# Queries and keys laid out by halves of the head pairs, the first block's tiles loaded two at a time into the rooms of late weights, alpha read by rows, two softmax buffers

## The chip, the core and the metric

The kernel runs on one core of one Trainium2 chip. The time is device microseconds of one launch. The kernel before was run three times: 926.99, 926.79 and 925.41 us, median 926.79. One more execution was profiled. The engines are called as the profile calls them: PE (TensorE, matmuls), DVE (VectorE), ACT (ScalarE), POOL (GpSimd) and SP (SyncE, which here only issues transfers).

## The reference

Attention over a band of 64 positions, 8 batches and 8 heads of width 64, and then a two-layer network with a leaky slope per hidden unit over all 4608 tokens. All values are fp32.

```
scores = scale * np.matmul(q, k.transpose(0, 1, 3, 2))
mask = (rel >= 0) & (rel < window)
scores = np.where(mask, scores, -1000000000.0)
scores = scores - np.max(scores, axis=-1, keepdims=True)
attn = np.exp(scores)
attn = attn / (np.sum(attn, axis=-1, keepdims=True) + 1e-09)
x = np.matmul(attn, v)                  # to [4608 tokens, 512]
h = x @ w_in                            # [4608, 2048]
g = np.maximum(h, 0.0) + alpha * np.minimum(h, 0.0)
out = g @ w_out                         # [4608, 512]
```

`w_in` and `w_out` arrive as 64-bit floats, read by the kernel as pairs of 32-bit words.

## The kernel before

**Tiles and blocks.** The 4608 tokens are 36 tiles of 128, in 9 blocks of 4. Each tile goes through `attend`, and each block through 16 `cell`s, one for each slice f of 128 hidden units. In the first block the slices f = 0 to 3 are done for tiles 0, 1 and for tiles 2, 3 apart.

**Attention of a tile** (`attend`). The heads are four pairs e; the token axis has two halves u of 64. Loads: two for keys (k, L314, 256 KB each), four for queries (q, L323, 64 KB each, in runs of 64 floats), two for values (v, L334, 256 KB each). SP issues all of them, save the four q of tile 0, which ACT issues. The rows 64u to 64u+63 of the k and q tiles hold the half u of the token axis, for all four pairs. Scores s (L350) are 16 products of 64x64 by 64x128 (32 entries in the profile); DVE adds the mask and takes the row maxima (L366, one for each pair and half, 8 for a tile); ACT does the exponentials (L372, 8); DVE the reciprocals rc (L383, L384); POOL scales the rows (L388). For the tiles 0 to 7 PE then turns the weights by transposes t (L405), and ACT or DVE copies them to pt (L410, L412); PE multiplies by v into av (L441), ACT rounds it to xh (L445), DVE makes the remainder xl (L448). From tile 8 on DVE does the turning.

**Weights** (`weights`). There are 32 of them to prepare once: 16 slices of w_in and 16 of w_out, in turn. For each: a fetch by SP of 512 KB (raw, L239), a step on the high words by ACT or DVE (two, L248 or L250), a shift on DVE (L255 or L258), a conversion of the low words on ACT (low, L263), a join on DVE (val, L267), an addition on POOL (L271), a rounding on ACT to the high part (L282), and a subtraction on POOL or DVE for the low part (L286). High and low part are kept all through the run in win_h, win_l, wout_h, wout_l.

**A cell** is the product h (L482; high by high, high by low, low by high), the slope on ACT and DVE (g, L488, L491), the split of g into gh (ACT, L496) and gl (POOL, in the first block also DVE, L500), and the product o (L515), which adds up over the 16 slices.

**What sets the order.** The kernel makes a list of steps with the engines that may do them, an expected duration, the steps that they need, and the buffers that they take and give back. `Plan.order` puts them in an order before the launch: it goes forward in time with these expected durations, and of the steps that could start next on an engine it takes the one whose latest useful time (`late`, worked back from the due times `want`) is first. The order of each engine is then fixed; an engine that meets an instruction whose data is not there waits, and all behind it waits. At most 8 transfers are in flight in the plan (`FLIGHT`).

**Buffers that matter here** (the `stock`). Two places each for k and q, one for v, one for the softmax tile w of 128 x 8 x 128 (a second one comes when the last raw weights are gone), one pt, with a second later, three for raw weights. The four kinds of weight parts are one tile each of 128 x 8192 floats.

**alpha** is read by ACT's queue with one element in a run (`"(f p) -> p f"`, 2048 runs of 4 bytes); DVE makes the signs from it in four steps (L565 to L568).

Of the kernel before, what the change touches and what calls it, by code (L numbers as in the profile page):

```python
# [143 lines left out]
PAIRS = 4  # L144
TURNS = (14, 2, 6, 10)
# [5 lines left out]
def banded_attention_then_prelu_ffn(  # L151
# [47 lines left out]
    alpha_sb = const.tile([P, NF], F32, name="alpha_sb")  # L199
# [4 lines left out]
    win_h = const.tile([P, NP, DFF], F32R, name="win_h")  # L204
    win_l = const.tile([P, NP, DFF], F32R, name="win_l")
    wout_h = const.tile([P, NF, E], F32R, name="wout_h")
    wout_l = const.tile([P, NF, E], F32R, name="wout_l")
# [3 lines left out]
    stock = dict(bank=[4, 5, 6, 7], o=[0, 1, 2, 3], q=["q0", "q1"], k=["k0", "k1"], v=["v0"], w=["w0"],  # L211
# [3 lines left out]
    stock.update({f"x{i}": [i] for i in range(RING)})  # L215
    plan = Plan(stock)
# [12 lines left out]
    def weights(c):  # L229
# [43 lines left out]
        def parts():  # L273
            v = d["val"].bitcast(F32)
            if odd:
                return v, wout_h[:, f, :], wout_l[:, f, :]
            fs = slice(f * P, (f + 1) * P)
            return v.rearrange("p (a b) -> p a b", a=NP), win_h[:, :, fs], win_l[:, :, fs]

        def high(_):  # L280
            v, hi, _ = parts()
            nc.scalar.copy(hi, v)  # L282

        def rest(e):
            v, hi, lo = parts()
            (nc.gpsimd if e == POOL else nc.vector).tensor_tensor(out=lo, in0=v, in1=hi.bitcast(F32),  # L286
                                                                  op=ALU.subtract)
# [7 lines left out]
        s6 = step({ACT: (0.51, 0.61)}, high, [s5])  # L295
        s7 = step({POOL: (1.22, 1.28), DVE: (1.15, 1.22)}, rest, [s6], give=[val])
# [6 lines left out]
    def attend(t, by_pe, want, loads_behind=(), behind=(), last=None):  # L303
# [3 lines left out]
        qb, kb, vb, wb, pb = Buffer("q", 1), Buffer("k", 1), Buffer("v", 1), Buffer("w", 2 if by_pe else 1), Buffer("pt", 1)  # L307
        loads, first_load = [], []
        for u in range(2):
            def load_k(_, u=u):  # L310
                if u == 0:
                    d["k"] = room(kb, [P, NP, 2, 2, W], F32, f"k_{t}")
                r = slice(u * D, (u + 1) * D)
                nc.sync.dma_start(d["k"][r].rearrange("d e b h w -> d e (b h w)"),  # L314
                                  kT[:, :, 2 * t + u:2 * t + u + 2].rearrange("e d b h w -> d e (b h w)"))
            loads.append(step({SP: (0.62, 0.62)}, load_k, (), [*loads_behind, *loads[:1]],
                              take=[kb] if u == 0 else [], moved=1.18))
        for u, h in ((0, 0), (0, 1), (1, 0), (1, 1)):
            def load_q(e, u=u, h=h):
                if u == h == 0:  # L320
                    d["q"] = room(qb, [P, NP, 2, W], F32, f"q_{t}")
                r = slice(u * D, (u + 1) * D)
                (nc.scalar if e == ACT else nc.sync).dma_start(  # L323
                    d["q"][r, :, h, :], qT[:, :, t, h, u * W:(u + 1) * W].rearrange("e d q -> d e q"))
            first_load.append(step({ACT if t == 0 else SP: (0.64, 0.64)}, load_q, (), [*loads_behind, *first_load[:1]],
                                   take=[qb] if u == h == 0 else [], moved=0.45))
        loads += first_load

        lv = []
        for u in range(2):  # L330
            def load_v(_, u=u):
                if u == 0:
                    d["v"] = room(vb, [P, NP, 2, P], F32, f"v_{t}")
                nc.sync.dma_start(d["v"][u * W:(u + 1) * W].rearrange("w c b d -> w c (b d)"),  # L334
                                  vN[:, :, 2 * t + u:2 * t + u + 2].rearrange("c w b d -> w c (b d)"))
            lv.append(step({SP: (0.62, 0.62)}, load_v, (), [*loads_behind, *lv[:1]], take=[vb] if u == 0 else [],
                           moved=1.18))
# [3 lines left out]
        def score(_):  # L341
            d["w"] = room(wb, [P, NH, KW], F32, f"w_{t}")
            for x in ("nm", "sm", "rc"):
                d[x] = sb.tile([P, NH], F32, tag=f"{x}{t % 2}", name=f"{x}_{t}")
            d["s"] = [bank(banks[u], [P, NP, KW], F32, f"s_{t}_{u}") for u in range(2)]
            for e in range(NP):
                for h in range(2):
                    for u in range(2):
                        r = slice(u * D, (u + 1) * D)
                        nc.tensor.matmul(d["s"][u][h * W:(h + 1) * W, e], d["q"][r, e, h, :], d["k"][r, e, :, h, :],  # L350
                                         start=True, stop=True)

        cold = 1.0 + 0.9 * (t < 2)
        sc = step({PE: (1.05 * cold, 1.15 * cold)}, score, loads, behind, take=[*banks, wb], give=[qb, kb])
# [92 lines left out]
        def x_low(_):  # L447
            nc.vector.tensor_tensor(out=xl[:, :, xs], in0=d["av"], in1=xh[:, :, xs].bitcast(F32), op=ALU.subtract)  # L448
            d.clear()
# [203 lines left out]
```

## Time and profile before

| | us |
|---|---|
| median of three runs | 926.79 |
| profiled execution | 927.84 |
| its span (first to last instruction) | 926.1 |
| PE busy | 895.6 (97%) |
| DVE busy | 452.2 (49%) |
| ACT busy | 383.8 (41%) |
| POOL busy | 310.3 (34%) |
| PE busy, 160 to 880 us | 720.00 of 720.00 |

The shares of busy time are means over two very different stages. In the first 160 us the weights are prepared and the first two blocks go through attention, and DVE, ACT and POOL have far more to do than later. From 160 us to about 918 us PE has no idle time that the profile shows. A row of a timeline gives the start and the length in us, the engine, the line, the operation, its output and inputs, the shape, how many, and in brackets the idle time of the engine before it with what ended it. A row of waits gives the engine and line that waited, for whom, the total in us, how often, and the longest.

### The profile page before, as it was taken

What the parts mean: (1) busy time and instruction counts of PE and PEld (TensorE: products, weight loads), DVE (VectorE), ACT (ScalarE), POOL (GpSimd) and SP (SyncE); (2) the same over time, 40 slices, a digit from 0 to 9 for tenths busy, and PEclk for the clock granted to TensorE, in tenths of its full rate; (3) what the DMA queues carried; (4) which work ended last, traced back from release to release, by engine and by line L of the source; (5) the groups of instructions that cost most, each with busy time, mean ns of one, the idle gap of its engine ahead of it and who ended that gap; (6) DMA issues with size and microseconds to landing.
All of it is one profiled execution on the core that took longest, in us unless ns stands there. A gap on an engine that the chain in (4) does not pass through costs nothing.

```text
span 926.1 us, 15516 instructions
## 1 busy us (share of the span) xinstructions
PE 895.6 (97%) x5872; PEld 730.0 (79%) x5872; DVE 452.2 (49%) x1317; ACT 383.8 (41%) x1020; POOL 310.3 (34%) x241
## 2 busy tenths in 40 slices
PE   3699999999999999999999999999999999999998
PEld 2578777888888888888888888888888888888886
DVE  3788996564454445444444444445444444421111
ACT  4677775433333334333333343334333433322222
POOL 3466874332333222233332233322333223322221
PEclk9999999999999999999999999999999999999999
DMA  9697756322232223111322232223222232001001
GB/s 217 171 225 198 215 158 124 96 58 57 58 104 52 54 49 97 51 45 48 100 58 57 58 103 58 58 58 103 58 57 59 57 103 57 1 1 46 1 1 46
DMA packets 96410, 74.41 MB, mean 80 GB/s; under 512 B 44624, under 2 KB 89680, under 8 KB 96336
## 3 DMA queue, kind: packets, MB, share of 16 engines
q1 hardware_dynamic: 93184, 73.16, 31.2%
q8 instruction: 46, 0.75, 0.3%
q10 hardware_dynamic: 3152, 0.27, 0.3%
q14 instruction: 28, 0.23, 0.1%
HBM read 63.97 MB, written 9.44 MB: 79 GB/s over the span
## 4 chain that ended last, share of the span: by engine, by line
PE 88%; DVE 6%; DMA 2%; issue 2%; POOL 1%; ACT 1%; SPq 0%; POOLq 0%; ACTq 0%; DVEq 0%
PE h L482 41%; PE o L515 40%; PE s L350 4%; PE av L441 4%; DVE w L366 1%; DVE val L267 1%; DMA raw<-w_out 1%; DMA raw<-w_in 1%; DVE gl L500 1%; DVE wout_l L286 1%; DVE two L255 1%; DMA q<-qT 1%; DVE two L250 1%; PE t L405 0%; POOL w L388 0%
## 5 line engine op out<-in xcount | busy, mean ns | idle before, releaser
L500 POOL TENSOR_TENSOR gl<-g,gh 128x512 fp32r<-128x512 f32 (+1 forms) x136 | 173.6, 1276 | 427.6 <-ACT gh L496 424.1
L491 DVE SCALAR_TENSOR_TENSOR g<-h,s_sb,g 128x512 f32<-128x512 f32 (+1 forms) x148 | 108.8, 735 | 290.2 <-ACT g L488 290.0
L488 ACT ACTIVATE g<-h,sa_sb 128x512 f32<-128x512 f32 (+1 forms) x148 | 100.3, 678 | 332.1 <-PE h L482 329.4
L515 PE MATMUL o<-wout_l,gh 128*128 128x512 f32 x576 | 226.6, 393 | 2.1 <-DVE wout_l L286 1.7
L515 PE MATMUL o<-wout_h,gh 128*128 128x512 f32 x576 | 226.7, 394 | 0.8 <-ACT gh L496 0.7
L426 DVE STREAM_TRANSPOSE pt<-w 32x256 f32<-32x256 f32 x336 | 146.6, 436 | 34.0 <-POOL w L388 29.2
L482 PE MATMUL h<-xh,win_h 128*128 128x512 f32 (+1 forms) x592 | 160.2, 393 | 1.8 <-DVE nm L366 1.2
L515 PE MATMUL o<-wout_h,gl 128*128 128x512 f32 x576 | 160.2, 391 | 0.6 <-POOL gl L500 0.4
L482 PE MATMUL h<-xl,win_h 128*128 128x512 f32 (+1 forms) x592 | 155.6, 385 | 0.0
L482 PE MATMUL h<-xh,win_l 128*128 128x512 f32 (+1 forms) x592 | 155.1, 384 | 0.0
L372 ACT ACTIVATE w<-w,nm 128x128 f32<-128x128 f32 x288 | 112.0, 392 | 59.5 <-DVE nm L366 59.5
L496 ACT CAST gh<-g 128x512 fp32r<-128x512 f32 (+1 forms) x148 | 90.0, 608 | 111.7 <-DVE g L491 109.6
L515 PEld LDWEIGHTS o<-wout_l,gh 128*128 128x128 f32 x576 | 108.2, 188 | 26.5 <-DVE wout_l L286 3.1
L515 PEld LDWEIGHTS o<-wout_h,gl 128*128 128x128 f32 x576 | 108.0, 188 | 25.3 <-POOL gl L500 0.9
L482 PEld LDWEIGHTS h<-xl,win_h 128*128 128x128 f32 x592 | 110.0, 189 | 22.5
L515 PEld LDWEIGHTS o<-wout_h,gh 128*128 128x128 f32 x576 | 108.2, 188 | 24.3 <-ACT gh L496 1.0
L482 PEld LDWEIGHTS h<-xh,win_l 128*128 128x128 f32 x592 | 109.9, 189 | 22.0
L482 PEld LDWEIGHTS h<-xh,win_h 128*128 128x128 f32 x592 | 107.1, 189 | 25.5 <-issue 2.1
L388 POOL TENSOR_TENSOR w<-w,rc 128x1024 f32<-128x1024 f32 (+1 forms) x44 | 70.7, 1609 | 152.3 <-DVE rc L384 142.7
L366 DVE CUSTOM_DVE_ANT_0 w<-s,masks 128x128 f32<-128x128 f32 x288 | 63.7, 286 | 63.6 <-PE s L350 63.5
L372 ACT ACTIVATION_READ_ACCUMULATOR w<-w,nm 128x1 f32 x288 | 54.6, 190 | 0.0
L350 PE MATMUL s<-k,q 64*64 64x128 f32 x1152 | 44.6, 292 | 7.9 <-DMA q<-qT 7.7
(44 smaller groups left out, 464.3 us busy)
## 6 DMA issues: line engine op xcount, KB each, us to landing
k<-kT SPq DMA_DIRECT2D x72, 256.0 KB, 4.1
v<-vN SPq DMA_DIRECT2D x72, 256.0 KB, 4.1
out<-os SPq DMA_DIRECT2D x36, 256.0 KB, 2.3
q<-qT SPq DMA_DIRECT2D x140, 64.0 KB, 3.4
raw<-w_in SPq DMA_DIRECT2D x16, 512.0 KB, 5.3
raw<-w_out SPq DMA_DIRECT2D x16, 512.0 KB, 4.7
q<-qT ACTq DMA_DIRECT2D x4, 64.0 KB, 5.4
alpha_sb<-alpha ACTq DMA_DIRECT2D x1, 8.0 KB, 5.9
```

The lines of the kernel that those rows point to most:

```text
L350: nc.tensor.matmul(d["s"][u][h * W:(h + 1) * W, e], d["q"][r, e, h, :], d["k"][r, e, :, h, :], start=True, stop=True)
L366: nc.vector.tensor_tensor_reduce(out=d["w"][:, g, :], in0=d["s"][u][:, e], in1=m, op0=ALU.add, op1=ALU.min, scale=-SCALE, scalar=3.0e38, a ...
L372: nc.scalar.activation(w, w, AF.Exp, scale=-1.0, bias=d["nm"][:, g:g + 1], accum_out=d["sm"][:, g:g + 1])
L388: nc.gpsimd.tensor_tensor(out=w, in0=w, in1=d["rc"][:, g].unsqueeze(2).broadcast_to(list(w.shape)), op=ALU.mult)
L426: nc.vector.transpose(d["pt"][ks, :, r], d["w"][r, :, ks])
L441: nc.tensor.matmul(av[r, e, u * W:(u + 1) * W], d["v"][:, e, u, r], d["pt"][:, u * NP + e, h * W:(h + 1) * W], start=True, stop=True)
L482: nc.tensor.matmul(ph[:, :nt], wt[:, c, fs], xt[:, c, xs], start=(k == 0), stop=(k == 3 * NP - 1))
L488: nc.scalar.activation(d["g"], d["h"][:, :nt], AF.Copy, scale=sa_sb[:, f:f + 1])
L491: nc.vector.scalar_tensor_tensor(out=d["g"], in0=d["h"][:, :nt], scalar=s_sb[:, f:f + 1], in1=d["g"], op0=ALU.mult, op1=ALU.max)
L496: nc.scalar.copy(d["gh"], d["g"])
L500: (nc.gpsimd if e == POOL else nc.vector).tensor_tensor(out=d["gl"], in0=d["g"], in1=d["gh"].bitcast(F32), op=ALU.subtract)
L515: nc.tensor.matmul(po[t][0], gt[:, i * P:(i + 1) * P], wt[:, f, :], start=(f == 0 and k == 0), stop=(f == NF - 1 and k == 2))
```

## The change

**Layout of q and k.** The rows 64x to 64x+63 of the tiles now hold the head pairs 2x and 2x+1, with all tokens of the tile (or two tiles) behind each other. A tile's q is two transfers with runs of 1 KB in place of four with 256 bytes; its k is two transfers of three blocks of 64 keys (384 KB in all), where the two halves before had two blocks each (512 KB). A score product still takes 64 rows by 64 queries by 128 keys; the two banks of scores now part the pairs and not the token halves.

**The first block two tiles at a time.** For tiles 0, 1 and for tiles 2, 3 one set of loads brings q, k and v of both: q 2 x 256 KB in runs of 2 KB, k 2 x 320 KB in runs of 2.5 KB, v 2 x 512 KB in runs of 2 KB. They land in rooms z0 to z3, which later become the parts of the weights with f = 12 to 15 of w_out and f = 11 to 15 of w_in (`LATE`); these parts are now tiles of their own, and the steps that write the first of each wait until the room is given back. ACT's queue issues the two k of tile 0 (behind alpha), SP all else.

**alpha by rows.** It is read as 16 rows of 512 bytes; PE turns it with one transpose (the first PE instruction, into one of the banks for o), and DVE reads it there.

**Two softmax buffers** w0 and w1 from the start.

The due time of the signs goes from 14 to 20; the high parts of a kind, and the low parts, are kept in order of f. The diff, cut to its core:

```diff
+LATE = (("wout_h", 12, "z0"), ("wout_l", 12, "z1"), ("win_h", 11, "z2"), ("win_l", 11, "z3"))
...
-    alpha_sb = const.tile([P, NF], F32, name="alpha_sb")
+    alpha_sb = const.tile([NF, P], F32, name="alpha_sb")
...
-    stock = dict(bank=[4, 5, 6, 7], o=[0, 1, 2, 3], q=["q0", "q1"], k=["k0", "k1"], v=["v0"], w=["w0"],
+    stock = dict(bank=[4, 5, 6, 7], o=[0, 1, 2, 3], q=["q0", "q1"], k=["k0", "k1"], v=["v0"], w=["w0", "w1"],
...
+    for _, _, z in LATE:
+        stock[z], stock["late " + z] = [z], []
...
-        s6 = step({ACT: (0.51, 0.61)}, high, [s5])
-        s7 = step({POOL: (1.22, 1.28), DVE: (1.15, 1.22)}, rest, [s6], give=[val])
+        prior = cv[c - 2]["done"] if c >= 2 else [None, None]
+        s6 = step({ACT: (0.51, 0.61)}, high, [s5], prior[:1] if prior[0] else [], take=late("_h"))
+        s7 = step({POOL: (1.22, 1.28), DVE: (1.15, 1.22)}, rest, [s6], prior[1:] if prior[0] else [],
+                  take=late("_l"), give=[val])
...
+        span = 2 if t < NBLK else 1
+        own = t % span
+        t0 = t - own
+        if own == 0:
+            if span == 2:
+                j = t // 2
+                qb = kb = Buffer(f"z{2 + j}", 2, f"late z{2 + j}")
+                vb = Buffer(f"z{j}", 2, f"late z{j}")
...
+            NW = 2 * span + 1
...
+                    nc.sync.dma_start(d["q"][r], qT[2 * x:2 * x + 2, :, t:t + span].rearrange("e d t h q -> d e (t h q)"))
...
+                    (nc.scalar if e == ACT else nc.sync).dma_start(
+                        d["k"][r], kT[2 * x:2 * x + 2, :, 2 * t:2 * t + NW].rearrange("e d b h w -> d e (b h w)"))
...
-                        nc.tensor.matmul(d["s"][u][h * W:(h + 1) * W, e], d["q"][r, e, h, :], d["k"][r, e, :, h, :],
-                                         start=True, stop=True)
+                            nc.tensor.matmul(d["s"][x][h * W:(h + 1) * W, u, y], q[r, y, own, h, u * W:(u + 1) * W],
+                                             k[r, y, 2 * own + u:2 * own + u + 2, h, :], start=True, stop=True)
...
-        nc.scalar.dma_start(alpha_sb, alpha.rearrange("(f p) -> p f", p=P))
+        nc.scalar.dma_start(alpha_sb, alpha.rearrange("(f p) -> f p", p=P))
+    def turn_alpha(_):
+        al["t"] = bank(ab, [P, NF], F32, "alpha_t")
+        nc.tensor.transpose(al["t"], alpha_sb, ident[:NF, :NF])
```

With other loads and buffers the plan comes out differently, on every engine, through the first two blocks. First place: SP's queue at the start of the program (k, q, v, qk are the attention's loads, raw the weights'; the number after a name is the tile's own). Before:

```order
L314 DMA k_95<-kT 64x4x256 x2
L314 DMA k_101<-kT 64x4x256 x2
L323 DMA q_106<-qT 64x4x64 x4
L334 DMA v_112<-vN 64x4x256 x2
L239 DMA raw_137<-w_in 128x4x256
L239 DMA raw_139<-w_in 128x4x256
L239 DMA raw_141<-w_out 128x1024
L314 DMA k_148<-kT 64x4x256 x2
L323 DMA q_159<-qT 64x4x64 x4
L239 DMA raw_219<-w_in 128x4x256
```

Now:

```order
L353 DMA qk_96<-qT 64x2x512 x2
L367 DMA v_101<-vN 64x4x512 x2
L249 DMA raw_104<-w_in 128x4x256
L353 DMA qk_108<-qT 64x2x512
L356 DMA qk_108<-kT 64x2x640
L353 DMA qk_108<-qT 64x2x512
L356 DMA qk_108<-kT 64x2x640
L249 DMA raw_117<-w_in 128x4x256
L249 DMA raw_141<-w_out 128x1024
L367 DMA v_173<-vN 64x4x512 x2
```

The loads of tiles 2 and 3 now stand ahead of the second raw weight; before, the first three raw weights stood ahead of tile 2's. Second place: DVE, from the end of the first masks to its first work on weights. Before (tile 0's last reciprocal, then the first weights, then the first mask of tile 1):

```order
L384 RECIPROCAL rc_118<-rc_118 128x4
L250 TENSOR_SCALAR two_183<-raw_137 128x512
L258 TENSOR_SCALAR two_183<-two_183 128x512
L267 SCALAR_TENSOR_TENSOR val_216<-raw_137,two_183 128x512
L258 TENSOR_SCALAR two_221<-two_221 128x512
L366 ISA w_194,nm_195<-s_0_198,masks 128x128
```

Now (the last mask of tile 1, whose softmax tile is w_143, then the first weight, with tile 0's copies of the turned weights, t_0 and t_1, between):

```order
L405 ISA w_143,nm_144<-s_1_148,masks 128x128
L405 ISA nm_144 128x1
L260 TENSOR_SCALAR two_206<-raw_104 128x512
L451 COPY pt_92<-t_0_195 128x512
L422 TENSOR_SCALAR rc_146<-sm_145 128x4
L423 RECIPROCAL rc_146<-rc_146 128x4
L268 TENSOR_SCALAR two_206<-two_206 128x512
L451 COPY pt_92<-t_1_214 128x512
```

Tile 1's eight masks have moved ahead of the first weight. Third place: DVE around the masks of tile 2. Before (w_309):

```order
L267 SCALAR_TENSOR_TENSOR val_291<-raw_141,two_260 128x512
L286 TENSOR_TENSOR win_l<-val_273,win_h 128x4x128
L412 COPY pt_92<-t_1_298 128x512
L258 TENSOR_SCALAR two_304<-two_304 128x512
L366 ISA w_309,nm_310<-s_0_313,masks 128x128
...
L267 SCALAR_TENSOR_TENSOR val_350<-raw_219,two_304 128x512
```

Now (w_251):

```order
L277 SCALAR_TENSOR_TENSOR val_245<-raw_104,two_206 128x512
L268 TENSOR_SCALAR two_273<-two_273 128x512
L487 TENSOR_TENSOR xl<-av_228,xh 128x4x128
L405 ISA w_251,nm_252<-s_0_255,masks 128x128
...
L265 TENSOR_SCALAR two_284<-two_284,flip_sb 128x512
L277 SCALAR_TENSOR_TENSOR val_329<-raw_117,two_273 128x512
```

One weight is joined ahead of tile 2's masks; before it was three (val_291 the third). The shift of the first w_out weight (two_284) stands right behind these masks, and all of DVE's later work behind it.

More of the change, by code (lines that the diff above doesn't have):

```diff
@@ L202, in banded_attention_then_prelu_ffn, with weight @@
     sa_sb = const.tile([P, NF], F32, name="sa_sb")
[L204 to L207, printed above, removed]
+    parts_of = {}
+    for name in ("win_h", "win_l", "wout_h", "wout_l"):
+        ends = sorted(f for n, f, _ in LATE if n == name)
+        parts_of[name] = {0: const.tile([P, ends[0], E], F32R, name=name)}
+    def weight(name, f):
+        f0 = max(x for x in parts_of[name] if x <= f)
+        return parts_of[name][f0][:, f - f0, :]
     xh = const.tile([P, NP, RING * P], F32R, name="xh")
     xl = const.tile([P, NP, RING * P], F32R, name="xl")
-    stock = dict(bank=[4, 5, 6, 7], o=[0, 1, 2, 3], q=["q0", "q1"], k=["k0", "k1"], v=["v0"], w=["w0"],
+    stock = dict(bank=[4, 5, 6, 7], o=[0, 1, 2, 3], q=["q0", "q1"], k=["k0", "k1"], v=["v0"], w=["w0", "w1"],
                  pt=["pt0"], new=[], g=["g0", "g1"], gh=["gh0", "gh1", "gh2"], gl=["gl0", "gl1"],
@@ L271, in total, with late, begin @@
             nc.gpsimd.tensor_tensor(out=d["val"], in0=d["val"], in1=d["tail"], op=ALU.add)
[L273 to L278, printed above, removed]
+        name = "wout" if odd else "win"
+        def late(part):
+            return [Buffer("late " + z, 1) for n, f0, z in LATE if (n, f0) == (name + part, f)]
+        def begin(part):
+            for n, f0, z in LATE:
+                if (n, f0) == (name + part, f):
+                    f1 = min([x for m, x, _ in LATE if m == n and x > f0], default=NF)
+                    parts_of[n][f0] = sb.tile([P, f1 - f0, E], F32R, tag=z, name=f"{n}_{f0}")
         def high(_):
-            v, hi, _ = parts()
-            nc.scalar.copy(hi, v)
+            begin("_h")
+            nc.scalar.copy(weight(name + "_h", f), d["val"].bitcast(F32))
         def rest(e):
-            v, hi, lo = parts()
-            (nc.gpsimd if e == POOL else nc.vector).tensor_tensor(out=lo, in0=v, in1=hi.bitcast(F32),
-                                                                  op=ALU.subtract)
+            begin("_l")
+            (nc.gpsimd if e == POOL else nc.vector).tensor_tensor(
+                out=weight(name + "_l", f), in0=d["val"].bitcast(F32), in1=weight(name + "_h", f).bitcast(F32),
+                op=ALU.subtract)
         s0 = step({SP: (0.4, 0.4)}, fetch, take=[raw], moved=1.3 if odd else 2.4)
@@ L306, in attend @@
         early = t < 2
[L307 to L337, printed above, removed]
+        wb, pb = Buffer("w", 2 if by_pe else 1), Buffer("pt", 1)
@@ L339, in attend @@
+        loads, lv, qb, kb, vb = st[t0]["from"]
         banks = [Buffer("o" if early else "bank", NP) for _ in range(2)]
@@ L366, in mask @@
                     nc.vector.tensor_tensor_reduce(
[L367 removed]
+                        out=d["w"][:, g, :], in0=d["s"][e // 2][:, u, e % 2], in1=m, op0=ALU.add, op1=ALU.min,
                         scale=-SCALE, scalar=3.0e38, accum_out=d["nm"][:, g:g + 1])
@@ L373, in soft @@
                                          accum_out=d["sm"][:, g:g + 1])
-                m = step({DVE: (0.21, 0.37)}, mask, [sc], give=[banks[u]])
+                m = step({DVE: (0.21, 0.37)}, mask, [sc], give=[banks[e // 2]])
                 some.append(step({ACT: (0.385, 0.58)}, soft, [m]))
@@ L479, in hidden @@
             k = 0
-            for wt, xt in ((win_h, xh), (win_h, xl), (win_l, xh)):
+            for wt, xt in (("win_h", xh), ("win_h", xl), ("win_l", xh)):
                 for c in range(NP):
-                    nc.tensor.matmul(ph[:, :nt], wt[:, c, fs], xt[:, c, xs],
+                    nc.tensor.matmul(ph[:, :nt], weight(wt, f)[:, c * P:(c + 1) * P], xt[:, c, xs],
                                      start=(k == 0), stop=(k == 3 * NP - 1))
@@ L513, in outs @@
                     po[t] = (bank(ob[t], [P, E], F32, f"o_{t}"), )
-                gt, wt = ((gh, wout_h), (gh, wout_l), (gl, wout_h))[k]
-                nc.tensor.matmul(po[t][0], gt[:, i * P:(i + 1) * P], wt[:, f, :],
+                gt, wt = ((gh, "wout_h"), (gh, "wout_l"), (gl, "wout_h"))[k]
+                nc.tensor.matmul(po[t][0], gt[:, i * P:(i + 1) * P], weight(wt, f),
                                  start=(f == 0 and k == 0), stop=(f == NF - 1 and k == 2))
```

61 lines of the change are left out of this document (47 added, 14 removed).

## The prediction

> **What bounds the kernel now.** I read the windows by stage first: start and end in us, its length, busy time and count of PE, PEld, DVE, ACT and POOL, PE's clock, DMA's share, GB/s.
>
> ```profile
> 0.00:10.50 10.50, 2.77 (x32) 2.13 (x32) 0.60 (x4) 1.28 (x1) 2.66 (x12) 1.00 0.93 146
> 10.50:56.60 46.10, 30.54 (x311) 24.09 (x310) 34.00 (x116) 32.99 (x102) 22.99 (x19) 1.00 0.81 206
> 56.60:148.20 91.60, 89.69 (x613) 72.03 (x614) 81.27 (x181) 67.31 (x164) 64.64 (x52) 1.00 0.73 188
> 160.00:880.00 720.00, 720.00 (x4665) 589.42 (x4664) 323.68 (x1002) 267.41 (x731) 206.93 (x149) 1.00 0.24 60
> 880.00:926.10 46.10, 41.49 (x181) 33.53 (x180) 6.64 (x9) 10.34 (x16) 10.07 (x8) 1.00 0.06 23
> ```
>
> From 160 to 880 us PE is full, and its products there are the same after the change: no time can be won or lost there, and the last stage (4.6 us without PE) has the same order in both. What can move is when PE reaches that stage. The borders: at 10.5 DVE begins its first mask, at 56.6 tile 3 is ready, at 148.2 the last weight is joined. Next, who PE waits for from 56 to 160 us, and the last such wait in the timeline:
>
> ```profile
> PE o L515 <- DVE wout_l L286: 1.7, 4, 0.7
> PE h L482 <- DVE xl L448: 0.5, 1, 0.5
> PE o L515 <- POOL wout_l L286: 0.3, 1, 0.3
> PE t L405 <- DVE rc L383: 0.2, 1, 0.2
> PE s L350 <- DVE val L267: 0.2, 1, 0.2
> 152.74 0.50 PE L515 MATMUL o<-wout_l,gh 128*128 128x512 f32 x1 [0.66 <-DVE wout_l L286]
> ```
>
> PE waits little (2.9 us), but for weights, from 98 us to the last one at 152.74. So two things end together: PE's own work, and the weights, whose work is on DVE (89% busy in the third row, 74% in the second). A gain needs both earlier. Now what stops DVE from 10.5 to 57 us:
>
> ```profile
> DVE w L366 <- PE s L350: 2.6, 2, 1.9
> DVE rc L383 <- ACT w L372: 2.3, 3, 1.2
> DVE two L250 <- DMA raw<-w_in: 1.9, 1, 1.9
> DVE pt L412 <- PE t L405: 1.9, 1, 1.9
> ```
>
> These are 8.7 of its 12.1 idle us.
>
> **The change, part by part.** *First scores.* Here are the first mask, the scores of one tile on a slow PE and the first weight step:
>
> ```profile
> 10.54 0.29 DVE L366 CUSTOM_DVE_ANT_0 w<-s,masks 128x128 f32<-128x128 f32 x1
> 16.42 0.69 DVE L250 TENSOR_SCALAR two<-raw 128x512 f32<-128x512 f32 x1 [1.95 <-DMA raw<-w_in]
> 17.09 1.99 PE L350 MATMUL s<-k,q 64*64 64x128 f32 x32
> ```
>
> The first scores now need 1.18 MB (two q of 0.262, two k of 0.328 MB), before 0.79 MB. What a MB costs, from two windows, 2 to 6.7 us (with its GB/s in 40 slices) and 14 to 18 us, and the median us from issue to landing of one store:
>
> ```profile
> DMA packets 1765, 0.99 MB, mean 210 GB/s; under 512 B 1003, under 2 KB 1765, under 8 KB 1765
> GB/s 0 0 61 166 192 148 139 218 253 257 381 347 312 327 255 227 251 242 166 194 216 229 196 212 240 201 246 248 231 201 231 220 222 183 216 203 205 203 187 190
> DMA packets 1084, 1.44 MB, mean 361 GB/s; under 512 B 46, under 2 KB 960, under 8 KB 1084
> out<-os SPq DMA_DIRECT2D x36, 256.0 KB, 2.3
> ```
>
> With mostly 256-byte packets it is 210 GB/s, with few of them 361. The new packets are of 2 to 2.5 KB: between these I take the second, as the nearer. The first bytes flow in the third slice, at 2.2 us, 1.4 us after the first issue at 0.8; I allow another microsecond for the landing (an estimate from that 1.4). So 2.2 + 1.18/0.361 + 1.0 = 6.5 us, and about 0.5 more because v, behind q on SP's queue, shares the engines with the last k: 7.0 (at 210 GB/s: 8.8). With 2.0 us of scores the first mask is at 9.0, against 10.54: **1.5 us** earlier, from 0 to 2.3. The two k cost ACT two issues, ahead of anything that it could do. Alpha: ACT issues it first, and it is 16 packets; even 256 KB land in 2.3 us when the engines are free (out), so alpha is there by 4 us, PE's transpose (a fraction of a microsecond) lies in its wait for q and k, and the four sign steps in DVE's idle start. Nothing for these; if alpha came after 7 us, all would move by the excess, since the transpose is first on PE.
>
> *Raw weights.* They now stand behind more bytes: the first ends at 2.75 MB of all that is asked for, the third at 4.97 MB (before 2.6 and 3.7 MB). At 361 GB/s they land at 2.2 + 7.6 + 1 = 10.8 and at 17.0 us; at 210 at 16.3 and 26.9. DVE, after 16 masks at a start-to-start of 0.21 us and two pairs of rc, asks for the first at 9.0 + 4.0 = 13.0 (16.42 before). The third is needed behind tile 2's masks, at about 9.0 + 13 = 22. I take no wait; the other end, 26.9, is a rival.
>
> *DVE from 9.0 to the eighth weight and tile 3.* Of the 46.1 us the wait for raw w_in (1.9) goes, and most of that for ACT's exponentials (2.3): with two softmax buffers there are masks of the next tile to do meanwhile. Of the 2.6 for scores I take 1 us off, since tile 1's now follow tile 0's at once. The w_out raw of 0.8 in the same list goes too. New is a wait for tile 0's xl, which now stands ahead of tile 2's masks: tile 0's av ends at about 9.0 + 9.5, its high part 0.6 later, while DVE is there at 9.0 + 8.6, so 1.5. Sum 1.9 + 2.1 + 1.0 + 0.8 - 1.5 = **4.3 us** less, so 42 of 46.1 (81% busy, between 74% and the third row's 89%; bounds 38.2 and 46.1).
>
> *DVE's load.* Counted in the order up to the last join, DVE has five high-word steps fewer (ACT does them), five copies to pt more, three subtractions of weights fewer, one half-size gl more. The rows of that stage:
>
> ```profile
> L250 DVE TENSOR_SCALAR two<-raw 128x512 f32<-128x512 f32 x16 | 11.0, 688 | 4.0 <-DMA raw<-w_out 2.1 <-DMA raw<-w_in 1.9
> L286 DVE TENSOR_TENSOR win_l<-val,win_h 128x512 fp32r<-128x512 f32 x8 | 9.6, 1197 | 2.7 <-ACT win_h L282 2.7
> L412 DVE COPY pt<-t 128x512 f32<-128x512 f32 x3 | 2.0, 683 | 1.9 <-PE t L405 1.9
> L286 POOL TENSOR_TENSOR wout_l<-val,wout_h x8: 1271/1287/1300, 29.5 to 146.4; 128x512 fp32r<-128x512 f32 x8
> ```
>
> -5 x 0.688 + 5 x 0.683 - 3 x 1.2 + 0.6 = -3.0, at 89% busy **3.4 us**. POOL takes the subtractions, at 1.29 each, and has 27 us free in that stage; ACT takes five steps and gives five copies back.
>
> *The sum for the weights*: 1.5 + 4.3 + 3.4 = 9.2 us earlier.
>
> *PE's side.* DVE's work ahead of tile 3's xl falls by 2 val, 3 shifts, 1 high-word step, 2 weight subtractions, 1 g, 2 gl, against 3 more pt copies: 1.36 + 2.1 + 0.69 + 2.4 + 0.5 + 1.2 - 2.05 = 6.2 us, of 34.0. So tile 3 is ready at 9.0 + (34.0 - 6.2)/0.81 = 43.3, 13.3 before the 56.6 of now. PE owes then one h and two o of two tiles more than now. From the chain of waits:
>
> ```profile
> 66.67 1.37 PE o L515 x6
> 71.22 1.43 PE h L482 x12
> ```
>
> That is 1.43 + 2 x 1.37 = 4.2, so it is 9.1 us ahead. Both sides give 9; since each will at times wait for the other (PE's 2.9 us above, with DVE as now), I take off 1: **8 us**.
>
> The second w costs nothing in the steady stage (from tile 8 on there were two already); the rooms are given back by tile 3's av, long before w_in's slice 11 is written (the 23rd of 32 weights, beyond 100 us).
>
> *The clock.* PE's groups are slow at first:
>
> ```profile
> 16.07 1.09 PE L405 MATMUL t<-ident,w 128*128 128x128 f32 x4 [0.77 <-ACT pt L410]
> 19.00 1.97 PE L441 MATMUL av<-pt,v 128*64 128x64 f32 x32
> 39.11 1.05 PE L482 MATMUL h<-xh,win_l 128*128 128x256 f32 x4
> 44.35 0.64 PE L482 MATMUL h<-xh,win_l 128*128 128x256 f32 x4
> ```
>
> From 16.07 to 20.97 PE works without a gap and stays slow; the same four products take 1.05 us at 39 and 0.64 at 44, after 5.6 us without a gap. The granted clock reads 1.00 all along, so only the durations tell. The walk above uses slow durations up to tile 1. [...]
>
> **The forecast.** The profiled execution took 927.84 us, 1.05 over the median of the runs: 927.84 - 8 = 919.8, and 918.8 beside the median of 926.79.
>
> **The rivals.** *A, the third raw weight is late (923.4).* DVE's order is fixed, and behind tile 2's masks stands the shift of the first w_out. At 210 GB/s it lands at 26.9, and with ACT's step ahead of it (0.6) DVE waits until 27.5, against 22: 5 us lost, and a good half of that is not made up (DVE is nearly full later). For it: 210 is what the first 5 us show, and q, k, v and weights now come without a pause for 6 MB. Against it: those are 256-byte packets. 8 - 4.6 = 3.4 us.
>
> *B, PE is quick from tile 1 on (915).* In the new order PE does av of tile 0, s of 2, t of 1, s of 3, av of 1 behind each other, about 10 us of work from 16 us on; the trace needed at most 5.6. Then t, s, av, t, h lose some 4 us by 26 to 30 us, as the pairs 1.05 and 0.64 show, and DVE's waits for PE (the 2.6 and 1.9 above) go. DVE at 89% from 9.0 on gives 38.2 in place of 42, and PE's side as much: 8 + 3.8 = 11.8. [...]
>
> *C, slower (929).* The same queue, at under 183 GB/s: the third raw then lands after 2.2 + 4.97/0.183 + 1 = 30.4, and the wait of over 8 us eats the whole lead. At 170 GB/s it is at 32.4, 2 us over, so 929. The window to 10.5 us has 146 GB/s as its mean, but it begins with 2.2 us of nothing and holds alpha's 2048 runs. It decides from 183 GB/s down.
>
> *D, no change (926.8).* The waits of DVE only move (from raw weights to xl and t), and PE's and the weights' ends stay tied at 152 us as now. Against it: 1.5 us at the start and 3.0 us of DVE work go in any case. Nothing else ties the change to its rooms (above), so that it doesn't do what it says has no chance of its own.
>
> **How the numbers follow.** Forecast 0.50 (916.5 to 921.5), A 0.21, B 0.15, C 0.07, D 0.07. Bounds of the terms: start 0 to 2.3, DVE's stage 0 to 7.9, load 3.4, less 0 to 2 for mutual waits; the ends of all at once are not likely. A range of 913 to 924.5 leaves out C, D and parts of A and B, together about 2 in 10. By 0.2%, 1.85 us, a measurement of this kernel can tell a difference from none: faster 0.87 (forecast, B, A, and a shade of D), same 0.06, slower 0.07.
>
> **What would show it.** First mask at 9.0 (8.2 to 10.5); DVE's first weight step at about 13 with no wait for raw; tile 3's xl at about 43; the last weight subtraction at about 143 to 145, and PE's last wait for wout_l with it; PE full behind it, and a last stage as before. Two rows would prove me wrong: DVE waiting for raw<-w_out around 22 to 27 us (A, C), or PE waiting for weights for over 6 us between 45 and 145 us, which would say that PE's lead is not worth anything without a quicker DVE. If t of tile 2 takes 0.6 us and not 1.1, it is B.

## The result, and the profile after

| | before | changed |
|---|---|---|
| median of the runs, us | 926.99 (925.41 to 927.80, 5 runs) | 921.84 (917.98 to 923.04, 5 runs) |
| ratio, with its 95% interval | | 0.9938 (0.9913 to 0.9962) |
| profiled execution, us | 927.84 | 917.98 |
| its span, us | 926.1 | 916.2 |
| PE busy, and the span less that, us | 895.6, 30.5 | 892.2, 24.0 |

The changed kernel is faster by 5.2 us of median, and the interval is clear of no change. The profiled execution is the quickest of its five and 9.9 us below that of before. Of these, 3.4 us are PE products that took less time (the number of products is the same but for one transpose, and the same product runs at a slow or at a quick pace: four t take 1.1 us or 0.66), and 6.5 us are time in which PE had nothing to do.

The windows of the changed kernel by the borders of the prediction (start, end, length, then busy time and count of PE, PEld, DVE, ACT, POOL, PE's clock, DMA's share, GB/s):

```profile
0.00:10.50 10.50, 1.76 (x19) 1.32 (x23) 0.60 (x4) 1.28 (x1) 2.65 (x12) 1.00 0.80 179
10.50:56.60 46.10, 36.70 (x417) 30.70 (x410) 38.41 (x140) 35.71 (x117) 28.22 (x24) 1.00 0.88 219
56.60:148.20 91.60, 89.82 (x602) 72.06 (x601) 75.94 (x160) 67.84 (x156) 65.82 (x51) 1.00 0.61 177
160.00:870.00 710.00, 710.00 (x4588) 580.13 (x4588) 318.23 (x978) 261.13 (x710) 200.95 (x145) 1.00 0.19 54
870.00:916.20 46.20, 42.07 (x183) 33.85 (x181) 6.64 (x9) 10.39 (x17) 10.31 (x8) 0.99 0.06 23
```

From 160 us on PE is full as before, and the last stage is the same. Nearly all of the idle time that is won lies in the second row: PE does 36.7 us of work there in place of 30.5, and 417 products in place of 311. The first row costs 1.0 us (1.76 us of work in place of 2.77). DVE in the third row is down from 81.3 to 75.9 us busy.

The waits of PE from 56 to 160 us, and DVE's last subtraction of a weight:

```profile
PE h L519 <- DVE val L277: 1.4, 2, 1.0
PE h L519 <- DVE g L528: 0.4, 1, 0.4
138.89 0.69 DVE L300 TENSOR_TENSOR wout_l<-val,wout_h 128x512 fp32r<-128x512 f32 x1
```

From 56 to 160 us PE no longer waits for wout_l at all. The weights, which ended together with PE's waiting at 152.7 us before, now end at 139.6, 13.1 us earlier and well clear of it.

The start, the second raw weight of w_in, and the end of the attention of the first block:

```profile
6.45 0.65 PE L388 MATMUL s<-qk 64*64 64x128 f32 x2 [2.65 <-DMA qk<-kT]
9.67 3.69 PE L388 MATMUL s<-qk 64*64 64x128 f32 x62 [2.57 <-DMA qk<-kT]
11.81 0.29 DVE L405 CUSTOM_DVE_ANT_0 w<-s,masks 128x128 f32<-128x128 f32 x1 [7.31 <-PE s L388]
22.30 0.63 ACT L258 ACTIVATE two<-raw 128x512 f32<-128x512 f32 x1 [3.34 <-DMA raw<-w_in]
22.96 0.70 DVE L268 TENSOR_SCALAR two<-two 128x512 int32<-128x512 int32 x1 [2.84 <-ACT two L258]
28.08 1.15 PE L480 MATMUL av<-pt,v 128*64 128x64 f32 x32
29.16 0.66 PE L444 MATMUL t<-ident,w 128*128 128x128 f32 x4
42.31 0.69 DVE L487 TENSOR_TENSOR xl<-av,xh 128x512 fp32r<-128x512 f32 x1 [0.31 <-ACT xh L484]
```

The first mask is 1.3 us later than before (10.54), not earlier: PE's scores wait for keys. A wait for a late raw weight is there, 2.8 us on DVE. PE's products are quick from 28 us on (v's 32 products in 1.15 us, 1.97 before at 19; t in 0.66), and tile 3 is ready at 43.0 (the end of its xl), 13.6 us ahead of before.

### The profile page after: what moved, and what is told of

The parts are those of the page before. It is cut to its first block, busy times and chain, and to the rows that moved or that the text cites. A ratio compares the mean times of both kernels' runs of the same rounds, so it can differ in the third digit from the quotient of the medians.

```text
span 916.2 us, 15392 instructions
## 1 busy us (share of the span) xinstructions
PE 892.2 (97%) x5873; PEld 727.5 (79%) x5873; DVE 445.6 (49%) x1315; ACT 382.7 (42%) x1020; POOL 313.6 (34%) x243
## 4 chain that ended last, share of the span: by engine, by line
PE 90%; DMA 3%; ACT 3%; DVE 2%; issue 1%; POOL 1%; POOLq 0%; SPq 0%; ACTq 0%; DVEq 0%
PE h L519 42%; PE o L552 41%; PE av L480 4%; PE s L388 3%; DMA raw<-w_in 1%; DMA qk<-kT 1%; DMA raw<-w_out 1%; PE t L444 1%; ACT w L411 1%; ACT low L273 0%; ACT win_h L296 0%; DVE val L277 0%; POOL val L281 0%; DVE two L260 0%; DVE win_l L300 0%
## 5 line engine op out<-in xcount | busy, mean ns | idle before, releaser
L281 POOL TENSOR_TENSOR val<-val,low 128x512 int32<-128x512 int32 x32 | 42.6, 1339 | 12.5 <-DVE val L277 8.4
```

Of the source, the lines that this page charges most:

```text
L281: nc.gpsimd.tensor_tensor(out=d["val"], in0=d["val"], in1=d["tail"], op=ALU.add)
```

## The experiments

Each edit below is one to the changed kernel unless it says so. Every edit of loads or buffers makes `Plan.order` plan the work of the first 160 us anew, on all engines: what is measured is an edit together with its order. "Tile 3 ready" is the start of its xl on DVE. The last stage is the same in all kernels, so that PE's busy time after 160 us tells how far behind each is at that point: the span is 164.1 to 165.0 us longer than it in every one of them. Beside the first result the kernels came in three groups, each timed beside the kernel before on the same chip (its medians 927.42, 926.94 and 926.94); the ratio is to that, so kernels of different groups are compared by it. The profiled values are of one execution, which can lie some us off the median.

| kernel | first mask | tile 3 ready | PE after 160 us | median | ratio (95%) |
|---|---|---|---|---|---|
| before | 10.54 | 55.96 | 761.49 | 926.99 | |
| changed | 11.81 | 42.31 | 752.07 | 921.84 | 0.9938 (0.9913–0.9962) |
| changed, again | 11.82 | 42.51 | 753.35 | 921.49 | 0.9935 (0.9921–0.9948) |
| one softmax buffer | 12.06 | 54.17 | 760.82 | 927.82 | 1.0007 (0.9994–1.0019) |
| one tile at a time | 8.54 | 46.99 | 761.27 | 924.45 | 0.9973 (0.9963–0.9983) |
| neither of the two | 8.55 | 50.32 | 751.78 | 920.15 | 0.9936 (0.9920–0.9952) |
| neither, and alpha as before | 10.36 | 53.58 | 758.19 | 922.30 | 0.9957 (0.9941–0.9973) |
| before, with alpha by rows | 10.62 | 54.09 | 755.72 | 924.23 | 0.9972 (0.9960–0.9983) |
| changed, alpha as before | 14.89 | 44.92 | 758.84 | 925.13 | 0.9983 (0.9970–0.9996) |
| 128 partitions | 11.12 | 42.73 | 751.91 | 918.17 | 0.9903 (0.9891–0.9916) |
| 128 partitions, k behind q | 8.66 | 40.42 | 749.41 | 915.61 | 0.9895 (0.9878–0.9912) |
| the same, one tile, one buffer | 7.57 | 50.58 | 751.86 | 916.76 | 0.9895 (0.9879–0.9911) |
| the same, one tile, two buffers | 7.82 | 45.40 | 756.95 | 922.76 | 0.9959 (0.9946–0.9973) |

### The changed kernel again

No edit. The question was where a gain of 8 in the sum, 9.9 in one execution and 5.2 of median comes from.

> The changed kernel unaltered, since its five executions spread from 917.98 to 923.04 us while the profiled one (917.98) is the quickest of them. Theory H (the clock): the executions differ in when PE becomes quick; in the profile the products of the turning of tile 2 take 0.66 us at 29 us, and a slower execution shows 1.1 us there and the quick products only later, with 2 to 5 us more before 57 us and nothing later. Rival (landing times): the loads at the start land later in a slow execution, the first mask stands after 12.5 us in place of 11.81, and PE's clock rises at the same place. Time 918 to 923 either way.

921.49 (919.26 to 922.25, 5 runs), so the 5 us are confirmed. Its profiled execution took 919.26. A third one, taken later:

> The changed kernel unaltered, one more profiled execution, since ten executions spread from 918.0 to 923.0 and the two profiled ones (917.98, 919.26) differ by 1.2 us, all of it between 43 and 67 us, where the granted clock of the second reads 0.90. Theory H (the clock's rise falls differently each time): if this execution is at 921 or more, it shows a granted clock below 1 or slow products somewhere up to 70 us, for a sum of its surplus, and from 70 us on the same durations. Rival: the surplus lies behind 160 us.

It took 923.84. Its PE waits from 56 to 160 us:

```profile
PE h L519 <- DVE val L277: 2.4, 2, 1.5
PE h L519 <- DVE g L528: 2.1, 2, 1.8
PE o L552 <- DVE wout_l L300: 0.4, 1, 0.4
PE t L444 <- ACT pt L449: 0.3, 1, 0.3
```

Against the quick execution its span is 5.9 us longer. PE is without work for 24.7 us before 160 us in place of 19.9, and 3.6 of these 4.8 us lie between 56.6 and 150; tile 3 was only 1.3 us later. So the same program ends between 918 and 924, and in these two executions the difference goes with how well DVE's val and g keep ahead of PE, with tile 3 ready at nearly the same time. Neither of the expected causes is there: t of tile 2 takes 0.66 us in all three executions, the first mask is at 11.81, 11.82 and 11.65, and the surplus lies in waits behind 56 us. What sets them from one execution to the next the traces don't settle. Early products differ in pace between the executions too (t of tile 0 took 1.12, 0.66 and 1.11 us).

### One softmax buffer, one tile at a time, neither

The two edits, apart and together:

```diff
-    stock = dict(... w=["w0", "w1"],
+    stock = dict(... w=["w0"],
```
```diff
-        span = 2 if t < NBLK else 1
+        span = 1
...
-        stock[z], stock["late " + z] = [z], []
+        stock[z], stock["late " + z] = [], [z]
```

> The changed kernel with one softmax buffer at the start, as before. If the two buffers are what lets tile 1's masks follow tile 0's, its masks go back behind tile 0's turning (about 4 us later for tile 1), and of the 5 us won in the median some 2 to 4 go: 923.5 to 926. Rival (the loads of two tiles are what counts, the softmax of a tile is over before the next needs it): within 1 us of 921.8.

> The changed kernel with every tile loaded by itself (q and k still by halves of the head pairs, alpha by rows, two softmax buffers; the late weights' rooms stay empty at the start). Theory (two tiles at once are what brings tiles 1 to 3 forward): tile 3 is ready at 50 us or later in place of 43, and most of the gain goes: 924.5 to 927. Rival (the layout with longer runs and the second softmax buffer carry it; the first scores then need only 0.65 MB and come 2 us earlier): 918 to 922, first mask at 8.5 to 9.5.

With one buffer the gain is gone (ratio 1.0007), which is more than the 2 to 4 us expected; PE's first 60 us then have this row in its waits:

```profile
PE t L444 <- POOL w L427: 11.8, 6, 3.8
```

With one tile at a time less than half of the gain is left (924.45), though tile 3 is ready at 46.99 and not beyond 50. Read alone, these two runs say that the change lives on both parts together, as the prediction has it. The next one says otherwise.

> The changed kernel with every tile loaded by itself and one softmax buffer: only the layout by halves of the pairs and alpha by rows are left. Theory J (the gain is of the two parts together: a tile's masks can only follow the last tile's when both its q and k and a softmax buffer are there): both missing is not worse than one missing, 926 to 928.5, the same as the kernel before. Rival (the parts add up: 3 us for the loads, 6 for the buffer): 930 to 932. Rival (layout and alpha have a gain of their own): below 925.

**920.15: without the two-tile loads and without the second buffer the gain is all there**, and tile 3 is 8 us later than in the changed kernel. Its first mask and tile 3's xl:

```profile
8.55 0.29 DVE L405 CUSTOM_DVE_ANT_0 w<-s,masks 128x128 f32<-128x128 f32 x1 [4.04 <-PE s L388]
50.32 0.68 DVE L487 TENSOR_TENSOR xl<-av,xh 128x512 fp32r<-128x512 f32 x1
```

Its last weights are earlier still (the last subtraction starts at 135.65, in the changed kernel at 138.89). So the early tile 3, on which the prediction's PE side rests, isn't what carries the time; the two parts together are worth nothing that these runs can tell (0.9936 against 0.9938 and 0.9935), and each by itself costs: the two-tile loads with one buffer 0.71% (1.0007 against 0.9936, 6.6 us), the second buffer with single tiles 0.37% (3.4 us).

Where some of these 3.4 us go is seen in the PE timeline of the kernel with one tile and two buffers, at 88 us:

```profile
87.67 1.07 PE L519 MATMUL h<-xh,win_l 128*128 128x512 f32 x4
91.63 0.66 PE L444 MATMUL t<-ident,w 128*128 128x128 f32 x4 [2.89 <-DVE val L277]
92.29 1.99 PE L519 MATMUL h<-xh,win_h 128*128 128x512 f32 x4
94.08 1.90 PE L519 MATMUL h<-xl,win_h 128*128 128x512 f32 x4
95.78 1.11 PE L519 MATMUL h<-xh,win_l 128*128 128x512 f32 x4
```

Tile 3 is ready 3.3 us ahead of the kernel with neither, but PE then stands 2.9 us for DVE, which is busy with a weight. By the kernel's list of steps it is not the weight's value that t needs: the join (val) gives back the bank in which `two` lay, and t takes one of the four banks. The next products run at the slow pace for nearly 4 us (1.99 and 1.90 for what takes 1.07). PE's granted clock (the third number from the end of a row of windows) shows it, and it shows a second such stretch, behind two short waits of 1.20 and 0.78 us:

```profile
91.60:96.00 4.40, 4.36 (x13) 3.39 (x14) 4.14 (x5) 2.71 (x5) 4.23 (x3) 0.61 0.65 186
123.40:127.00 3.60, 3.57 (x9) 2.86 (x10) 2.82 (x5) 1.70 (x4) 3.49 (x3) 0.56 0.63 199
```

Over the whole execution, PE's busy time is 900.4 us against 892.7 of the kernel with neither, and its time without work 25.1 against 23.8: of the 9 us between these two executions 7.7 are slow products and only 1.3 idle time. These two executions lie further apart than the medians do (927.43 is 3.0 above the median of its kernel, 918.48 is 1.7 below), so part of the 9 us, perhaps the second stretch, belongs to the execution and not to the edit. Some of the slow products stand at the start. The groups of the score products up to 40 us, of the kernel with neither and of this one (busy us, mean ns, then the waits):

```profile
L388 PE MATMUL s<-k,q 64*64 64x128 f32 x128 | 7.7, 387 | 2.0 <-DMA k<-kT 2.0
```
```profile
L388 PE MATMUL s<-k,q 64*64 64x128 f32 x128 | 9.5, 424 | 4.0 <-DMA k<-kT 3.0 <-DVE xl L487 1.0
```

With two buffers these products come in more pieces with pauses between, and take 1.8 us more.

### alpha

The kernel with neither part, with alpha read as before; and the kernel before with only alpha by rows (and PE's transpose):

```diff
-        nc.scalar.dma_start(alpha_sb, alpha.rearrange("(f p) -> f p", p=P))
+        nc.scalar.dma_start(alpha_sb, alpha.rearrange("(f p) -> p f", p=P))
...
-    a1 = step({PE: (0.2, 0.4)}, turn_alpha, [a0], take=[ab])
```

> The kernel with single-tile loads and one softmax buffer, and alpha read as before the change (2048 runs of 4 bytes): against the kernel before, only the layout of q and k by halves of the pairs is left (and the plan's order that comes with it). Theory L (the layout brings the gain: half as many and four times longer runs, a quarter fewer bytes of k): the ratio stays near that of the kernel with both parts, 0.994 to 0.996, so 921 to 923. Theory A (alpha's runs hold up the start, and alpha by rows brings most of the gain, as its 3.4 us in the changed kernel suggest): 924 to 927, first mask about 3 us later than the 8.55 of the kernel with alpha by rows, at 10.5 to 12.

> The kernel before, with alpha by rows and PE's transpose as its only change (the order is planned anew). Theory A: the loads of the first tile are no longer beside 2048 runs of 4 bytes, first mask 1.5 to 2 us earlier than 10.54 and about 3 us off the time: 923 to 925. Theory L: the first mask comes earlier, but the runs of 256 bytes and the 25% more bytes of k keep what follows late: 925.5 to 928, within 0.2% of before.

Both have a part. The layout alone gives 922.30 (0.43% off), alpha by rows alone 924.23 (0.28% off), and the two together 920.15 (0.64% off): they add up within their intervals. So of the change's four parts these two make the gain; to the layout belong here the order of its plan, the late weights' own tiles and the fixed order of f, which stay in that kernel. The step that I expected of alpha failed, though: in the kernel before it doesn't bring the first mask forward (10.62). There alpha is not ahead of the first loads. ACT issues it behind tile 0's four q, and in the changed kernel first of all (the kernel before, the same with alpha by rows, the changed one):

```profile
3.84 0.62 ACTq L562 DMA_DIRECT2D alpha_sb<-alpha  x1
3.54 0.62 ACTq L562 DMA_DIRECT2D alpha_sb<-alpha  x1
0.81 0.40 ACTq L599 DMA_DIRECT2D alpha_sb<-alpha  x1
```

What it does bring is bytes. The window from 2 to 9.5 us, of the kernel before and of that with alpha by rows:

```profile
DMA packets 4362, 1.34 MB, mean 178 GB/s; under 512 B 3357, under 2 KB 4362, under 8 KB 4362
```
```profile
DMA packets 3251, 1.57 MB, mean 210 GB/s; under 512 B 2211, under 2 KB 3251, under 8 KB 3251
```

0.23 MB more have moved by 9.5 us. Its last join of a weight on DVE starts at 142.05, that of before at 148.19; how much of that is the earlier bytes and how much the new order isn't parted.

> The changed kernel with alpha read as before, 2048 runs of 4 bytes, and no transpose. If alpha by rows is worth nothing (it lies in DVE's idle start), within 1 us of 921.7. Rival (the 2048 runs take the engines' time from q and k, which are what the first scores wait for; before, GB/s fell to 30 to 60 for about a microsecond around 7.5 us): first mask about a microsecond later than 11.8 and 922.5 to 923.5.

In the changed kernel alpha's 2048 runs cost 0.45% by the ratios (0.9983 against 0.9938, 4.2 us; 3.3 by the medians), more than either theory gave, and 3.1 us of the first mask. The row of PE's first products:

```profile
12.76 3.69 PE L388 MATMUL s<-qk 64*64 64x128 f32 x62 [4.25 <-DMA qk<-kT]
```

The two k of the first tile that ACT's queue issues stand behind alpha there, and these 62 products start at 12.76 and not at 9.67. The prediction had put nothing on alpha.

### What a MB costs at the start

q and k are loaded by one transfer over all 128 partitions in place of two over 64, and v likewise. The arrays in memory are arranged so that the rows of both pairs lie behind each other (v twice, shifted by one block); the products and their results are the same.

```diff
-            for x in range(2):
-                r = slice(x * D, (x + 1) * D)
-                    nc.sync.dma_start(d["q"][r], qT[2 * x:2 * x + 2, :, t:t + span].rearrange("e d t h q -> d e (t h q)"))
+                nc.sync.dma_start(d["q"], qT[:, :, t:t + span].rearrange("y p t h q -> p y (t h q)"))
```

> The changed kernel with q, k and v each loaded by one transfer over all 128 partitions, in place of two over 64 (the arrays in memory are laid out so that both halves follow each other; same bytes, same runs). In the trace the loads at the start move at 180 to 250 GB/s though their packets have 2 KB; the stretches above 340 GB/s are those in which weights (128 partitions) or both halves are under way. Theory P (a transfer into 64 partitions reaches only about half the rate, 215 GB/s): q and k of the first two tiles are there by 6 to 7.5 us in place of 9.7, the first mask at 8 to 9.5 in place of 11.8, GB/s above 300 in the first 10 us, and the second w_in does not keep DVE waiting for 2.8 us: 3 to 5 us less, 917 to 919. Rival S (the 16 engines or the memory give about 220 GB/s at the start whatever the shape, or v's share of them is what delays k): first mask within 0.7 us of 11.8, 921 to 923.

The window from 2 to 9.5 us, of the changed kernel, of that with neither part, and of this one:

```profile
DMA packets 814, 1.66 MB, mean 221 GB/s; under 512 B 68, under 2 KB 69, under 8 KB 814
```
```profile
DMA packets 1477, 1.62 MB, mean 216 GB/s; under 512 B 148, under 2 KB 1477, under 8 KB 1477
```
```profile
DMA packets 1522, 2.66 MB, mean 354 GB/s; under 512 B 64, under 2 KB 507, under 8 KB 1522
```

In this window transfers into 64 partitions moved at nearly the same rate whether their packets were of 256 bytes and 1 KB mixed (210 above; two thirds of the packets have 256 bytes, but only a third of the bytes), of 1 KB (216) or of 2 KB (221). With 128 partitions and runs mostly of 2 KB and more it is 354. So for the changed kernel's loads the length of the runs was not what made them slow. That it was the partitions is likely, but not shown by itself: the edit also halves the number of transfers and puts the arrays in another order in memory. And 128 partitions alone did not bring the rate in every run. The kernel with 128 partitions and one tile at a time (its time is below), with runs of 1 to 1.5 KB, has these rows for 2 to 9.5 us and for 4 to 6.5 us:

```profile
DMA packets 1967, 2.17 MB, mean 289 GB/s; under 512 B 97, under 2 KB 1967, under 8 KB 1967
DMA packets 474, 0.55 MB, mean 219 GB/s; under 512 B 32, under 2 KB 474, under 8 KB 474
```

From 4 to 6.5 us the kernel with neither part moves 223 GB/s with 64 partitions, so there is no difference in that stretch. Yet the weights of 14 to 18 us in the kernel before, mostly 1 KB runs over 128 partitions, went at 361. What sets the rate there stays open. 918.17 is 3.3 us below the changed kernel on the same chip.

The first mask came only 0.7 us earlier, against the expectation (8 to 9.5): k of tile 0 was on ACT's queue, beside v and a weight on SP's, and its products start at 8.97. With it on SP's queue, right behind q:

```diff
-            loads.append(step({ACT if t == 0 else SP: (0.62, 0.62)}, load_k, (), [*loads_behind, *loads[-1:]],
+            loads.append(step({SP: (0.62, 0.62)}, load_k, (), [*loads_behind, *loads[-1:]],
```

> As the kernel with single transfers over 128 partitions (918.17), but the first k is issued by SP straight behind q, ahead of v and the first weight, in place of ACT's queue, where it shared the engines with them and landed at 8.9 us. If the start is on the path: q and k land at 6.3 to 7 us, the first mask is at 8.4 to 9.2 in place of 11.1, and the time falls by about as much, 915 to 917. Rival (from 46 us on PE is full and before that it waits for ACT, POOL and DVE in turn, so that the start is made up for later): first mask as said, time within 1 us of 918.2.

The first mask comes 2.5 us earlier, at 8.66, and the median is 915.61, the lowest of all. What these 2.5 us bring isn't shown, though: the medians are 2.6 us apart, but the ratios, 0.9903 and 0.9895, have intervals that overlap almost wholly.

### Again without the two parts

> Loads over 128 partitions, first k right behind q on SP's queue, alpha by rows, as in the best kernel so far (915.6), but one tile at a time and one softmax buffer. Only 0.65 MB have to land ahead of the first scores, not 1.18: at 354 GB/s 2.2 + 1.8 + 1 = 5.0, and with 2.0 of scores a first mask at 7.0 to 7.5 (8.66 in the best so far). Theory S (the start carries the time, two tiles at once and two buffers bring nothing of their own): 913.5 to 916. Rival T (with quick loads the two-tile loads and the second buffer are worth something, since PE then gets its second tile's scores at once): 917 to 920, with tile 3 ready later than the 40.4 us of the best so far.

> As the kernel before it in this list, with a second softmax buffer. With the narrow loads the second buffer went with 4.3 us more (924.45 against 920.15). Theory O (that was the planned order, not the buffer): here the difference is of another size or sign, within 2 us of the one with one buffer. Theory B (a second buffer with single-tile loads lets masks run ahead of the weights on DVE, and PE then waits for the weights): again 3 to 5 us more, with PE waiting for DVE's val or wout_l for over 4 us between 60 and 160 us.

With the quick loads it is the same picture. One tile and one buffer: 916.76 (0.9895), as the best (0.9895); the first mask is 1.1 us earlier still and tile 3 is 10 us later, and neither shows in the time. That lies between what the two theories gave (up to 916, and from 917) and by the time a little nearer to the one by which the two parts are worth something; the ratios, of which each is to the kernel before on its own chip, show no such worth. One tile and two buffers: 6.0 us more, again with PE standing for val, at the same place of the program:

```profile
89.35 0.66 PE L438 MATMUL t<-ident,w 128*128 128x128 f32 x4 [2.93 <-DVE val L277]
90.01 1.64 PE L513 MATMUL h<-xh,win_h 128*128 128x512 f32 x4
91.45 1.91 PE L513 MATMUL h<-xl,win_h 128*128 128x512 f32 x4
93.16 1.47 PE L513 MATMUL h<-xh,win_l 128*128 128x512 f32 x4
```

PE's granted clock from 89.3 to 95 us is 0.70. So the loss by a second buffer with single tiles comes back with other loads. The kernel of 915.61 and that of 916.76 beat both kernels of the case, the changed one by 0.4% of the ratio (0.9895 against 0.9938 and 0.9935).

## Why the prediction was right, and where it wasn't

918.8 was forecast and 921.84 measured: the direction, and the size within the range; the gain was 5.2 of 8. The reasons behind it were right in part only, and that the sum came this near is partly luck: by the runs the gain comes from the layout and from alpha, and the sum gave alpha nothing and the layout no price of its own.

- **First mask at 9.0: wrong, 11.81.** The step that failed is the price of a MB, "with few of them 361 ... between these I take the second, as the nearer". The 361 GB/s of 14 to 18 us were mostly weights, which fill 128 partitions; I put the difference to the length of the packets, and packets of 2 KB into 64 partitions moved at 221. The same walk at the lower bound of 210 gives 8.8 + 2.0 = 10.8. The rest is likely v, for which the sum had 0.5 us: by 9.5 us SP's queue had moved 1.00 MB, and only 0.52 of them are the two q.
- **Alpha: "Nothing for these": wrong.** 3 to 4 us in the changed kernel, 2.7 in the kernel before. That the transfer lands early was right (PE's transpose is at 3.51); that 2048 runs hold up the other loads, and what it is worth to be rid of them, was left out of the sum.
- **Raw weights, no wait: wrong in small.** DVE lost 2.8 us through ACT for the second w_in, as in rival A, but for another weight than A named.
- **Tile 3 at 43.3: right (43.0), by two errors that cancel.** The start was 2.8 us later than said, and the stretch from it to tile 3 3.1 us shorter (31.2 in place of 34.3): DVE had 26.0 us of work in it and not 27.8, and 5.2 us without work and not 6.5. PE's products ran quick from 28 us on, and t of tile 2 took 0.66 us, which is rival B's sign, while the sum had slow durations up to tile 1 and counted nothing for quicker ones behind it. How much of the shorter waits is that, the runs don't part; B's 915 did not come with its sign.
- **The weights 9.2 us earlier: right in kind, and the size lies between the executions.** The last subtraction starts 12.4 us earlier in the quick execution (138.89 for 151.33) and 6.5 in the slowest one profiled (144.80).
- **"Both sides give 9": the step that failed.** The runs show that tile 3's time isn't a bound of its own. 8 us earlier or later (42.31 against 50.32) and 10 us (40.42 against 50.58), the time is the same. In the kernel with one tile and two buffers PE's lead is spent in waits for DVE's val and in the slow products behind them; with one buffer and two-tile loads it is lost before, in PE's 11.8 us for POOL up to 60 us. What counts in each is how much PE loses in idle time and in slow products up to 160 us. The second row that would prove the prediction wrong (PE waiting for weights for over 6 us between 45 and 145 us) came true nowhere: the largest such sum here, for val, is 4.3 us, in a kernel with one tile and two buffers. It leaves out the slow products, which made 7.7 of the 9 us between the two executions above.
- **The parts.** The sum gave the gain to the two-tile loads and the second buffer. The runs give it to the layout of q and k (a quarter fewer bytes of k and transfers with runs of 1 KB, with the order that comes with it; which of these, isn't parted) and to alpha by rows. The two-tile loads delay the first mask by 3.3 us (8.55 to 11.81), and the second buffer makes that good.
- **PE full behind it, the last stage as before: right**, 710.00 of 710.00 us.

Open stays why the changed kernel's executions spread over nearly 6 us (917.98 to 923.84), what sets the rate of the first loads, and, since each edit makes a new plan, how much of any part is its transfers or buffers and how much the order that the planner then found.

## What to carry to other kernels

Before a rate is taken from another stretch of the trace, ask whether its transfers are like the new ones in more than the length of their packets, in the partitions that they fill, their number and the order of the arrays in memory: here loads mostly with packets of 2 KB moved at 221 GB/s into 64 partitions, and at 354 in half as many transfers into 128. A tile that was ready 8 us earlier was worth nothing here (42.31 against 50.32 us, ratios of 0.9938 and 0.9936), and with one tile and two buffers the lead went in PE's waits for val (4.2 us) and in slow products (1.99 and 1.90 us for 1.07), so price a lead only up to the next wait, and with such slow products where the trace has them. Where several parts go in together, leave out all of them but one, too: undoing one part at a time showed here two parts that seemed to carry everything and that together were worth nothing.

## What the runs showed of the hardware

- From 2 to 9.5 us, with alpha by rows, transfers into 64 partitions moved at 210 to 227 GB/s, with packets of 256 bytes and 1 KB mixed (210), of 1 KB (216) and of 2 KB (214 to 227); into 128 partitions at 354 and 359 with two-tile loads and at 289 with single tiles and one buffer, with 219 from 4 to 6.5 us.
- 2048 runs of 4 bytes, 8 KB in all, held back the loads queued behind them by 3.1 us in the changed kernel (products at 12.76 for 9.67) and cost 3 to 4 us of its whole time.
- Behind a wait of 2.9 us PE fell back to the slow pace for 3.5 and 4.4 us, in two kernels (1.99 and 1.90 us for 1.07 at a granted clock of 0.61; 1.64, 1.91 and 1.47 at 0.70). A wait of 1.92 us was followed by none (the kernel with neither part and alpha as before, at 87 us), two waits of 1.20 and 0.78 us close together by one (0.56).
- Two executions of one program differ in the pace of the same early products (t of tile 0 took 0.66 us in one, 1.12 and 1.11 in two others), and in their end by up to 6 us.
